# First tiles of a hash attention: full-height tables for the low parts, and another order of copies and loads

## Chip, core and metric

One NeuronCore of one Trainium2 chip runs the whole program. The metric is the device time of one execution in microseconds (us). Three executions of the kernel before took 699.73, 700.44 and 702.56 us; the median is 700.44 us.

## What is computed

Attention over 2 batches and 8 heads, 768 positions of 64 numbers each, where a query sees a key only if both fall into the same of 64 hash buckets; then two feed-forward blocks over the 1536 tokens. Cut to what matters here:

```
q_bits = (q @ proj > 0); k_bits = (k @ proj > 0)      # 6 bits
mask   = bucket(q_bits) == bucket(k_bits)
scores = where(mask, q @ k.T / 8, -1e9)
attn   = softmax(scores) ; x = attn @ v               # per head
x = (silu(x @ w_gate) * (x @ w_val)) @ w_out           # 512 -> 1536 -> 512
h = x @ w_in ; x = layernorm(h * softmax(h)) * g_ln @ w_out2
```

The feed-forward weights are 64-bit floats in memory and are turned to 32 bits by VectorE.

## The kernel before

**Numbers in two parts.** A float32 operand is kept as a rounded "high" part and a "low" rest, and products are summed from the parts. So each head's queries and keys, once transposed, stand in 128-row tiles: `kt` and `qa` hold high parts in rows 0 to 63 and low parts in rows 64 to 127. The score matmuls (`scores`, L515 to 528) read four other tiles: `ka` (the keys' high part twice), `qa`, `qb` (queries' high part, under it first the keys' high part and then the hash bits) and `kb` (the keys' low part, under it the hash bits).

**Pairs and slots.** Heads go in 8 pairs. A pair has 12 slots; slot i does one block of 128 queries against all 768 keys: `scores(i+1)`, `maxima(i)` and `biases(i)` on VectorE (DVE), `exps(i)` on ScalarE (ACT), the transposes of slot i-2 on TensorE (PE), their high and low parts on ACT and DVE (`highs`, `lows`), and the product with the values for slot i-5. `scores(i+1)` needs the PSUM buffer of `scores(i-1)`, so it starts after `exps(i-1)`. The order of all instructions is written by hand in the loop L797 to L847 and kept on each engine.

**Hashes of the first pair.** `first_hashes(j)` (L381 to 422) does one head at a time: 8 matmuls (L393) into two PSUM banks, four each, alternating between a table over all 128 rows (`hash_k`, `hash_q`) and one over the upper 64 rows only (`hash_first`, `hash_low`, rows `up`). Head 0 is done before the first score (in `start`), head 1 in slot 2, right behind the transposes of slot 0. DVE turns the sums into bits (L419, L403).

**Hashes of the other pairs.** `hashes(p, n)` (L467 to 494) does both heads of a pair in 6 matmuls (L483), three tables by two heads, all of 128 rows; the third table, `hash_low`, reads `qb`, in whose rows 0 to 63 lie the queries' high parts and in rows 64 to 127 the keys' high parts. They are put there by DMAs: `turn(p, j, g)` (L430 to 465) transposes a head's queries and keys in three groups, ACT copies them out, and for g = 1 four copies go out on SyncE's (SP's) DMA queue, `qb<-kt`, `ka<-kt` twice and `kb<-kt`, for g = 2 one more, `qb<-qa`. Each is 64 rows of 768 float32, 192 KB. For pair 1 these are the slots 3 to 6 of pair 0 (`beginning`), and its hashes are in slots 8 and 9. Slot 9's bits then go by four small DMAs (L494) into `qb` and `kb`; the first score of pair 1 is issued in slot 11.

**Loads and splits.** `load` (L232) brings a pair's queries, keys or values (384 KB each) on the same SP queue, into buffers of which there is one for each kind, so a load waits until GpSimd (POOL) has split the one before. In pair 0 the loads of pair 2's keys and queries, pair 1's values, pair 3's keys and queries stand in slots 2, 4, 6, 8, 10 (L770). POOL splits pair 1's keys and queries and pair 0's values by heads in 12 steps (`split_heads`, `opening`), of which one is taken in `start` and 2, 1, 2, 2, 2, 2 in slots 0 to 5 (L837).

**First weights.** `early` (L752) loads the first columns of `w_gate` and `w_val` (512 KB each) and converts them in 6 DVE steps each (L47 to L64). Its 14 steps are taken one before the loop (the first load, L789) and then one in each of the slots 3, 9 and 11 of every pair (L846) until they are done. The result is read when the attention has ended.

Of the kernel before, what the change touches and what calls it, by code (L numbers as in the profile page):

```python
# [9 lines left out]
F32 = mybir.dt.float32  # L10
# [57 lines left out]
def hash_attention_then_two_mlps(  # L68
# [116 lines left out]

    def window(w, g, rows=slice(0, P)):

        tile, start, _ = w
        return tile[rows, start - g * GR:start - g * GR + P]

# [17 lines left out]
    def hash_tables():  # L208
        start = hash_q[1]
        hash_fill(hash_q)  # L210
        nc.gpsimd.tensor_sub(pl, pj, hash_q[0][:, start:start + NB].bitcast(F32))
        hash_fill(hash_k, hash_first, hash_low)

    with at:
# [8 lines left out]

        hash_first = hash_weights(xs, "hash_first", 1, 3, (up, 0, 1, pl), tag="xf", bufs=3)
        one = sm.tile([P, 1], F32, tag="one", name="one", bufs=1)
# [155 lines left out]
        def first_hashes(j):  # L381
# [6 lines left out]
            for n in range(2):  # L388
                for m, (w, g, nm, rows) in enumerate((
                    (hash_k, 1, "kt", both), (hash_first, 1, "kt", up),  # L390
                    (hash_q, 0, "qa", both), (hash_low, 0, "qa", up),
                )):
                    nc.tensor.matmul(  # L393
                        t[n][:, :HALF], window(w, 2 * j + g, rows),
                        x[nm][rows, n * HALF:(n + 1) * HALF],
                        start=m == 0, stop=m == 3,
                    )
# [26 lines left out]
        def tiles_of_head():  # L424
# [3 lines left out]
            }  # L428

        def turn(p, j, g, bank=None):  # L430

# [21 lines left out]
            if g == 0:  # L453
                nc.scalar.mul(kt[:, 0:512], t, qscale)
            elif g == 1:
                nc.scalar.mul(kt[:, 512:S], t[:, 0:S - 512], qscale)
                nc.scalar.copy(qa[:, 0:1024 - S], t[:, S - 512:512])
                for dst, src in (
                    (qb[D:P], kt[0:D]), (ka[0:D], kt[0:D]), (ka[D:P], kt[0:D]),
                    (kb[0:D], kt[D:P]),  # L460
                ):
                    nc.sync.dma_start(dst.bitcast(F32), src.bitcast(F32))
            else:
                nc.scalar.copy(qa[:, 1024 - S:S], t)
                nc.sync.dma_start(qb[0:D].bitcast(F32), qa[0:D].bitcast(F32))

# [297 lines left out]
        def splitting(p, l):  # L764


            loads = {6: ((p + 3, "k"),), 9: ((p + 3, "q"),), 0: ((p + 1, "v"),)}
            at = {2: "k", 4: "k", 5: "q", 8: "q", 10: "v", 11: "v"}
            if p == 0:
                loads = {  # L770
                    2: ((p + 2, "k"),), 4: ((p + 2, "q"),), 6: ((p + 1, "v"),),
                    8: ((p + 3, "k"),), 10: ((p + 3, "q"),),
                }
                at = {6: "k", 7: "k", 8: "q", 9: "q", 10: "v", 11: "v"}
            for of in loads.get(l, ()):
                load(*of)
            nm = at.get(l)
            if nm:
                if nm not in splits:
                    splits[nm] = split(p + 1 if nm == "v" else p + 2, nm)  # L780
                    go(splits[nm])
                else:
                    go(splits.pop(nm))

        with tc.manual_schedule():
            for p, nm in ((1, "k"), (1, "q"), (0, "v")):
                load(p, nm)
            first_weights = early()
            go(first_weights)  # L789
            opening = (  # L790
# [6 lines left out]
            for i in range(NSLOT + 9):  # L797
# [38 lines left out]
                if i < 6:  # L836
                    for _ in range((2, 1, 2, 2, 2, 2)[i]):  # L837
                        go(opening)
# [4 lines left out]
                if part == 1:  # L843
                    go(done)
                    sums(h + 1)
                if l in (3, 9, 11):  # L846
                    go(first_weights)  # L847
# [397 lines left out]
```

## Time and profile before

| | us |
|---|---|
| median of three executions | 700.44 |
| the profiled execution | 700.14 |
| its span, first to last instruction | 698.30 |
| PE busy | 689.4 (99%) |
| DVE busy | 555.3 (80%) |
| ACT busy | 339.5 (49%) |
| POOL busy | 149.4 (21%) |

The rows that follow the change are of this one profiled execution. Times are from the start of the span. PE is matmuls, PEld the loading of their weights, SPq the DMA issues on SyncE's queue. "PEclk" is TensorE's granted clock as a share of 2.4 GHz. In a timeline row, the first number is the start, the second the time taken (of all the instructions merged into it, their count behind the x), and in brackets stands how long the engine sat idle before and what ended the wait. A matmul's given duration includes its way through the array; two that follow each other closely are better read by the distance of their starts.

### The profile page before, as it was taken

Reading aid. Unit: us, or ns where it says so; the run is one execution under the profiler, and the core shown is the slowest. Engines: PE = TensorE matmul, PEld = TensorE weight load, DVE = VectorE, ACT = ScalarE, POOL = GpSimd, SP = SyncE. Lnnn points to the kernel's source line nnn. Section 1 sums busy time; section 2 is a strip of 40 time slices with the busy share of each in tenths; the row PEclk is TensorE's granted clock in tenths of the full one; section 3 lists DMA queues with packets and bytes.
Section 4 is the critical chain, followed back from the end, with each engine's and each line's share of the span. In section 5 each row is a group of like instructions: output and inputs, shape, how many; then the busy total and the mean of one; then the engine's idle time right before and its main releaser. Section 6 shows DMA issues by size and latency. Waiting matters only on the chain.

```text
span 698.3 us, 10092 instructions
## 1 busy us (share of the span) xinstructions
PE 689.4 (99%) x3683; PEld 592.8 (85%) x3683; DVE 555.3 (80%) x979; ACT 339.5 (49%) x676; POOL 149.4 (21%) x156
## 2 busy tenths in 40 slices
PE   8899999999999999999999999999999999999998
PEld 5789999999999988888888888888888888888887
DVE  6779999999989998766786886977988976645552
ACT  6868989889898963433213122032123432222221
POOL 5626566555644260000000000000000000000000
PEclk9999999999999999999999999999999999999999
DMA  6745746446261403231313131131221000000001
GB/s 188 180 129 128 177 113 164 125 123 162 55 153 39 143 13 120 72 110 61 116 65 119 62 120 62 60 122 60 80 103 61 1 6 25 16 30 16 31 15 46
DMA packets 36177, 60.59 MB, mean 87 GB/s; under 512 B 4984, under 2 KB 26552, under 8 KB 35616
## 3 DMA queue, kind: packets, MB, share of 16 engines
q1 hardware_dynamic: 36128, 59.95, 29.7%
q8 instruction: 29, 0.48, 0.3%
q14 instruction: 20, 0.16, 0.1%
HBM read 36.71 MB, written 3.15 MB: 57 GB/s over the span
## 4 chain that ended last, share of the span: by engine, by line
PE 97%; ACT 2%; DMA 1%; issue 0%; DVE 0%; ACTq 0%
PE h L992 28%; PE s L524 10%; PE h L1104 10%; PE t L574 9%; PE y L1017 5%; PE y L1018 5%; PE y L1016 5%; PE av L609 5%; PE av L613 4%; PE o L1161 3%; PE o L1162 3%; PE o L1163 3%; PE pp L483 2%; PE t L1143 2%; PE pp L445 1%; DMA qb<-qa 1%
## 5 line engine op out<-in xcount | busy, mean ns | idle before, releaser
L992 PE MATMUL h<-xh,hi 128*128 128x512 f32 x288 | 112.2, 390 | 0.0
L992 PE MATMUL h<-xl,hi 128*128 128x512 f32 x288 | 112.2, 390 | 0.0
L992 PE MATMUL h<-xh,lo 128*128 128x512 f32 x288 | 111.3, 390 | 0.0
L587 DVE TENSOR_TENSOR el<-t,eh 128x384 fp32r<-128x384 f32 x192 | 97.9, 551 | 10.7 <-ACT eh L583 8.9
L559 ACT ACTIVATE e<-s,nm 128x768 f32<-128x768 f32 x96 | 97.9, 1020 | 4.4 <-PE s L524 2.2
L583 ACT CAST eh<-t 128x384 fp32r<-128x384 f32 x192 | 84.1, 495 | 25.3 <-PE t L574 23.9
L1130 POOL TENSOR_TENSOR w<-w,half 128x1 f32<-128x1 f32 x12 | 6.6, 550 | 416.2 <-DVE w L1129 322.0
L535 DVE TENSOR_REDUCE top<-s 128x1 f32<-128x768 f32 x96 | 90.7, 945 | 2.2 <-PE s L524 2.0
L574 PE MATMUL t<-idr,e 128*128 128x128 f32 x576 | 80.6, 275 | 0.0
L574 PEld LDWEIGHTS t<-idr,e 128*128 128x128 f32 x576 | 68.7, 141 | 8.7 <-DVE el L587 2.8
L609 PE MATMUL av<-eh,vs 128*128 128x384 f32 x186 | 64.6, 347 | 0.0
L992 PEld LDWEIGHTS h<-xh,hi 128*128 128x128 f32 x288 | 54.1, 188 | 11.2
L992 PEld LDWEIGHTS h<-xl,hi 128*128 128x128 f32 x288 | 54.1, 188 | 11.1
L992 PEld LDWEIGHTS h<-xh,lo 128*128 128x128 f32 x288 | 54.0, 188 | 11.1
L1002 ACT CAST ah<-sg 128x512 fp32r<-128x512 f32 x36 | 22.4, 622 | 74.6 <-DVE sg L1000 74.6
L524 PE MATMUL s<-ka,qa 128*128 128x384 f32 x192 | 55.4, 370 | 1.1 <-ACT e L559 1.1
L1017 PE MATMUL y<-al,hi 128*128 128x512 f32 x144 | 56.1, 390 | 0.0
L1018 PE MATMUL y<-ah,lo 128*128 128x512 f32 x144 | 56.1, 390 | 0.0
L1016 PE MATMUL y<-ah,hi 128*128 128x512 f32 x144 | 56.1, 390 | 0.0
L1000 DVE TENSOR_TENSOR sg<-h,sg 128x512 f32<-128x512 f32 x36 | 24.8, 690 | 37.0 <-PE h L992 22.0
L613 PE MATMUL av<-el,vs 128*64 128x384 f32 x155 | 52.8, 340 | 0.0
L963 ACT CAST hi<-wf 128x1024 fp32r<-128x1024 f32 x17 | 17.8, 1050 | 69.8 <-DVE wf L64 69.8
(212 smaller groups left out, 1427.9 us busy)
## 6 DMA issues: line engine op xcount, KB each, us to landing
raw<-in_moe_w_out_dram SPq DMA_DIRECT2D x10, 1024.0 KB
raw<-in_moe_w_gate_dram SPq DMA_DIRECT2D x12, 512.0 KB
raw<-in_moe_w_val_dram SPq DMA_DIRECT2D x12, 512.0 KB
ka<-kt SPq DMA_DIRECT2D x30, 192.0 KB
raw<-in_moe_w_in_dram SPq DMA_DIRECT2D x4, 1024.0 KB
v<-in_v_dram SPq DMA_DIRECT2D x8, 384.0 KB
kb<-kt SPq DMA_DIRECT2D x15, 192.0 KB
qb<-qa SPq DMA_DIRECT2D x15, 192.0 KB
```

Source lines behind the costliest of these rows:

```text
L524: nc.tensor.matmul(s[:, n, :HALF], a[:, rows], m[:, n * HALF:(n + 1) * HALF], start=first, stop=not first,)
L535: nc.vector.tensor_reduce(top[:, 1:2], s_of[i][:, :, :HALF], AX.XY, ALU.max, negate=True)
L559: nc.scalar.activation(e, s_of.pop(i)[:, :, :HALF], AF.Exp, bias=nm[:, 1:2], scale=nm[:, 0:1], accum_out=total_of[p, n][:, j, c:c + 1],)
L574: nc.tensor.transpose(t[:, m, :], e_of[i][:, g, m * P:(m + 1) * P], idf)
L583: nc.scalar.copy(half_tile(eh_of, i, g), t_of[i, g])
L587: last_of[i] = nc.vector.tensor_sub(half_tile(el_of, i, g), t_of.pop((i, g)), half_tile(eh_of, i, g).bitcast(F32),)
L609: nc.tensor.matmul(av, vj[:, c], eh_of[h][:, c, :], start=c == 0, stop=c == C - 1)
L613: nc.tensor.matmul(*low, start=False, stop=False)
L992: nc.tensor.matmul(ps[n], a[:, n, kk, :], x[:, kk, blk * BLK:(blk + 1) * BLK], start=kk == 0 and a is hi and x is xh, stop=kk == KD - 1 an ...
L1016: nc.tensor.matmul(p, hi[:, cols], ah, start=f == t * FT, stop=False)
L1017: nc.tensor.matmul(p, hi[:, cols], al, start=False, stop=False)
L1018: nc.tensor.matmul(p, lo[:, cols], ah, start=False, stop=f == (t + 1) * FT - 1)
```

## The change

The tables of the low parts for the first pair become two tiles of 128 rows, `hash_first["k"]` and `hash_first["q"]`, zero in rows 64 to 127, and all 8 matmuls of `first_hashes` read 128 rows. Of pair 1's copies, the three that `turn` issues for `ka` and `kb` of each head are kept in a list and issued behind the last `qb<-qa` of the pair. The loads in pair 0 move to slots 1, 4, 7, 9, 11. The splits' steps are taken 2, 1, 3, 2, 2, 1. The first load of `early` is not issued before the loop, and its steps are taken in slots 3, 9, 11 of pair 2 and later.

```diff
-    def window(w, g, rows=slice(0, P)):
+    def window(w, g):
         tile, start, _ = w
-        return tile[rows, start - g * GR:start - g * GR + P]
+        return tile[:, start - g * GR:start - g * GR + P]
...
-        hash_fill(hash_k, hash_first, hash_low)
+        hash_fill(hash_k, hash_first["k"], hash_first["q"], hash_low)
...
-        hash_first = hash_weights(xs, "hash_first", 1, 3, (up, 0, 1, pl), tag="xf", bufs=3)
+        hash_first = {
+            nm: hash_weights(xs, f"hash_first_{nm}", n, n + 2, (up, 0, n, pl), tag="xf", bufs=3)
+            for n, nm in enumerate("qk")
+        }
...
-                for m, (w, g, nm, rows) in enumerate((
-                    (hash_k, 1, "kt", both), (hash_first, 1, "kt", up),
-                    (hash_q, 0, "qa", both), (hash_low, 0, "qa", up),
+                for m, (w, g, nm) in enumerate((
+                    (hash_k, 1, "kt"), (hash_first["k"], 1, "kt"),
+                    (hash_q, 0, "qa"), (hash_first["q"], 0, "qa"),
                 )):
                     nc.tensor.matmul(
-                        t[n][:, :HALF], window(w, 2 * j + g, rows),
-                        x[nm][rows, n * HALF:(n + 1) * HALF],
+                        t[n][:, :HALF], window(w, 2 * j + g),
+                        x[nm][:, n * HALF:(n + 1) * HALF],
...
+        held = []
...
-                for dst, src in (
-                    (qb[D:P], kt[0:D]), (ka[0:D], kt[0:D]), (ka[D:P], kt[0:D]),
-                    (kb[0:D], kt[D:P]),
-                ):
-                    nc.sync.dma_start(dst.bitcast(F32), src.bitcast(F32))
+                move(qb[D:P], kt[0:D])
+                keys = [(ka[0:D], kt[0:D]), (ka[D:P], kt[0:D]), (kb[0:D], kt[D:P])]
+                if p == 1:
+                    held.extend(keys)
+                else:
+                    for dst, src in keys:
+                        move(dst, src)
             else:
                 nc.scalar.copy(qa[:, 1024 - S:S], t)
-                nc.sync.dma_start(qb[0:D].bitcast(F32), qa[0:D].bitcast(F32))
+                move(qb[0:D], qa[0:D])
+                if p == 1 and j == 1:
+                    for dst, src in held:
+                        move(dst, src)
...
                 loads = {
-                    2: ((p + 2, "k"),), 4: ((p + 2, "q"),), 6: ((p + 1, "v"),),
-                    8: ((p + 3, "k"),), 10: ((p + 3, "q"),),
+                    1: ((p + 2, "k"),), 4: ((p + 2, "q"),), 7: ((p + 1, "v"),),
+                    9: ((p + 3, "k"),), 11: ((p + 3, "q"),),
                 }
...
             first_weights = early()
-            go(first_weights)
...
-                    for _ in range((2, 1, 2, 2, 2, 2)[i]):
+                    for _ in range((2, 1, 3, 2, 2, 1)[i]):
                         go(opening)
...
-                if l in (3, 9, 11):
+                if p > 1 and l in (3, 9, 11):
                     go(first_weights)
```

## Rows read from the trace of the kernel before

**Rows 1.** The page, part 1: busy time, share of the span, instructions.

```profile
PE 689.4 (99%) x3683; PEld 592.8 (85%) x3683; DVE 555.3 (80%) x979; ACT 339.5 (49%) x676; POOL 149.4 (21%) x156
```

**Rows 2.** What PE waited for over the span: total us, times, longest.

```profile
PE pp L483 <- DMA qb<-qa: 3.2, 1, 3.2
```

**Rows 3.** Timeline of PE: pair 1's hashes and the scores behind them.

```profile
32.49 0.34 PE L483 MATMUL pp<-kt,hash_k 128*128 128x384 f32 x1
36.05 0.41 PE L483 MATMUL pp<-qb,hash_low 128*128 128x384 f32 x1 [3.23 <-DMA qb<-qa]
...
41.00 0.51 PE L524 MATMUL s<-ka,qa 128*128 128x384 f32 x2
...
46.15 0.51 PE L524 MATMUL s<-kb,qb 76*128 76x384 f32 x2
```

**Rows 4.** PE by stretches: us, PE busy (count), PEclk, DMA share, GB/s.

```profile
37.00:38.00 1.00, 1.00 (x5) 0.50 0.28 92
```

**Rows 5.** Timeline of PE: pair 2's hashes, the same instructions as rows 3.

```profile
62.70 0.33 PE L483 MATMUL pp<-kt,hash_k 128*128 128x384 f32 x1
62.87 0.33 PE L483 MATMUL pp<-qb,hash_low 128*128 128x384 f32 x1
...
66.14 0.51 PE L524 MATMUL s<-ka,qa 128*128 128x384 f32 x2
```

**Rows 6.** Stretch: PE, PEld, DVE, ACT, POOL busy; PEclk, DMA share, GB/s.

```profile
25.00:30.00 5.00, 4.87 (x34) 4.64 (x35) 4.10 (x8) 4.99 (x14) 3.26 (x4) 1.00 0.99 245
```

**Rows 7.** Timeline of PE: head 0's hashes, k transposes, first score.

```profile
6.17 0.41 PE L393 MATMUL pp<-kt,hash_k 128*128 128x384 f32 x1 [0.23 <-ACT kt L346]
6.51 0.43 PE L393 MATMUL pp<-kt,hash_first 64*128 64x384 f32 x1
...
9.10 0.88 PE L333 MATMUL t<-idr,first_ks 128*128 128x128 f32 x6
...
10.54 0.84 PE L524 MATMUL s<-kb,qb 76*128 76x384 f32 x2
```

**Rows 8.** Timeline of DVE: first load's wait, bits, first maximum, head 1's bits.

```profile
3.17 0.36 DVE L304 CAST first_ks<-first_k 128x384 fp32r<-128x384 f32 x1 [0.67 <-DMA first_k<-in_k_dram]
...
7.72 0.67 DVE L419 TENSOR_SCALAR kb<-pp,over,weigh 12x384 fp32r<-12x384 f32 x1 [0.40 <-PE pp L393]
...
9.21 0.67 DVE L419 TENSOR_SCALAR kb<-av,over,weigh 12x384 fp32r<-12x384 f32 x1 [0.26 <-PE av L393]
11.42 0.96 DVE L535 TENSOR_REDUCE top<-s 128x1 f32<-128x768 f32 x1 [1.54 <-PE s L524]
...
18.27 0.69 DVE L403 TENSOR_SCALAR bits<-av,over,weigh 64x384 fp32r<-64x384 f32 x1 [0.23 <-PE av L393]
```

**Rows 9.** Timeline of ACT: behind head 1's hashes, and pair 1's last copy.

```profile
19.49 0.86 ACT L583 CAST eh<-t 128x384 fp32r<-128x384 f32 x2 [1.86 <-PE t L574]
...
21.24 1.04 ACT L559 ACTIVATE e<-s,nm 128x768 f32<-128x768 f32 x1
...
27.91 0.68 ACT L464 CAST qa<-pp 128x512 fp32r<-128x512 f32 x1
```

**Rows 10.** DMA issues on SP's queue: start, time to issue.

```profile
14.55 0.46 SPq L286 DMA_DIRECT2D qb<-qa  x1
...
29.79 0.97 SPq L465 DMA_DIRECT2D qb<-qa  x1
...
42.74 0.77 SPq L286 DMA_DIRECT2D kb<-bits  x1
```

**Rows 11.** DMA share and GB/s of one stretch (PEclk first).

```profile
16.50:17.00 0.50, 1.00 0.10 25
```

**Rows 12.** The same queue: first bits copy of pairs 4, 5 and 6.

```profile
127.10 0.79 SPq L286 DMA_DIRECT2D qb<-bits  x1
...
157.00 0.79 SPq L286 DMA_DIRECT2D qb<-bits  x1
...
186.63 0.80 SPq L286 DMA_DIRECT2D qb<-bits  x1
```

## The prediction, made blind

> **What bounds the kernel now.** I read the busy times first: PE works 99% of the span [rows 1], so the time can only fall where PE waits, or where it is busy with less than it could do. What it waited for shows one long wait: the third table's matmul of pair 1's hashes, for the copy `qb<-qa` [rows 2]. The timeline there shows it: five matmuls follow at about 0.175 us, the fifth at 32.49, the sixth at 36.05 instead of 32.66 [rows 3], 3.4 us late. Behind the wait PE's clock is granted at half, 1.2 instead of 2.4 GHz [rows 4]. From the sixth matmul to the first score behind the second group takes 4.95 us (36.05 to 41.00) [rows 3]; the same instructions in the next pair, at full clock, take 3.27 us (62.87 to 66.14) [rows 5]. So the wait costs 3.4 us and 1.7 us more.
>
> Before the wait, in slots 3 to 8, ACT is the bound: 4.99 us of 5 busy, the DMA engines at 99% and 245 GB/s [rows 6]. Before that, PE is busy with little: the 8 matmuls of `first_hashes` start 0.34 to 0.38 us apart (6.17, 6.51, to 9.10 for the next work) [rows 7], those of `hashes`, as wide, 0.17 us [rows 5]. What differs is that each second one of the first uses 64 rows. Behind 41 us PE is without gaps, and what arrives there earlier arrives earlier at the end.
>
> **The change part by part.** The sum is made against the profiled execution, 700.14 us (span 698.30, 1.84 around it); the median of the three runs is 0.30 above it.
>
> *Tables of 128 rows, head 0.* Eight matmuls take 2.93 us (6.17 to 9.10) [rows 7]; at 0.175 us [rows 5] they take 1.4, so PE is 1.5 us ahead. DVE can't follow all the way: of its waits for these sums, 0.40 and 0.26 us fall away [rows 8], so its bits are done at 9.22 instead of 9.88. Score 0's second half needs the last of them; it starts at 9.3 instead of 10.54 [rows 7]. The maximum started 0.88 us behind that (11.42) [rows 8], with PE at half speed: the two matmuls there take 0.84 us, later ones 0.51 [rows 7, 3]. At half speed again the maximum comes at 10.2, 1.2 us earlier; at full speed at 9.8, 1.6 earlier. The slow end is the row itself; I take 1.3, between 1.0 and 1.6.
>
> *The same tables, head 1.* Again 1.5 us less on PE. Behind them ACT had idled 1.86 us for the transposes [rows 9], so it starts 1.5 earlier. But DVE's second set of bits waited only 0.23 us for PE [rows 8], so it comes only that much earlier, at 18.04 to 18.73, and pair 1's first transposes, which go into the same bank, wait for it: 18.8 us, then 0.4 for them and 0.8 for ACT's last two copies ahead of its exponential, which starts at about 20.1 instead of 21.24 [rows 9]. Taken: 1.2, between 0.9 and 1.5. All of this is in the old time scale; the 1.3 of head 0 comes on top. From here to 33 us ACT has no gap to lose it in [rows 6], so slots 3 to 8 move up by 2.5 us.
>
> The price of the tables is a DVE memset like the three beside it, in DVE's 0.67 us of waiting for the first load [rows 8], and one more small POOL block ahead of `hash_low`, which the first pair no longer reads. POOL's low part of head 0's successor slips by the length of one such block, and has its reader, the transposes, at 7.6 instead of 9.10 [rows 7]; it is ready by then. Without this cover it would be some 0.2 us. The two tiles take two of the three `xf` buffers until slot 2, the first `xf` is written in slot 8: nothing.
>
> *The copies and loads.* The last `qb<-qa` was issued at 29.79 [rows 10], 1.2 us behind the end of ACT's copy at 28.59 [rows 9], since SP was still issuing key copies; and it landed 6.3 us later, since everything in front of it had to go first. From the load in slot 2 on, these were 2 loads of 384 KB, 6 key copies and, with itself, 4 `qb` copies of 192 KB: 2688 KB. The change leaves 1152 KB of them: the 4 `qb` copies and one load. The missing 1536 KB take 6.4 us at 245 GB/s [rows 6]. By the queue alone the copy lands at 29.6 in the old scale; by its issue, at 28.59 and with the 2.1 us that a lone copy took (issued at 14.55, the engines idle from 16.6 on) [rows 10, 11], at 30.7. Its reader is due at 32.66. Both scales move up by 2.5 us alike, so a margin of 2 us stays, and the 3.4 us go altogether; with them the 1.7 us of half clock. Bounds: 0 to 5.1; I take all, because the margin is as large as a lone copy's whole time.
>
> *What is late next.* The 6 held copies are issued behind it, some 0.7 us each, from 26.7 to 31 in new time, and behind them on SP wait pair 1's values and `low<-xf`, neither read for several slots. 1152 KB and the load take 6.4 us, and are through at about 34.6. Pair 1's first score reads `kb` at 46.15 [rows 3], in new time 38.5. Ahead of it lie only slot 9's bits: `kb<-bits` was issued at 42.74 [rows 10], 3.4 us before its reader, and keeps this distance. So 3 us of room, and nothing charged; if it is gone, PE stands at that score.
>
> *Moved steps.* The key load of slot 1 is issued when POOL has split the keys before, and SP's next issue, head 1's bits, waits longer. A POOL step moves from slot 5 up to slot 2, where POOL waits for the next bias anyway. The conversions leave pairs 0 and 1 and come into pairs 5 and 6: a pair with three of them took 29.90 us, the next, without, 29.63 [rows 12]. As many leave as come; 0, between -0.5 and +0.5. The second of the weights' loads now has only slots 9 to 11 of pair 4 to land in, near 5 us against 2.1 and its transfer; if that is too little, DVE stands for up to 1 us.
>
> Sum: 1.3 + 1.2 + 3.4 + 1.7 = 7.6, so 692.5 beside the profiled run, and with 0.3 for the median 692.8.
>
> **The rivals.** *Height does not matter.* The eight matmuls stay 0.37 us apart, because the cause is something else, the two banks for one, and the 2.5 us don't come. For it: no row shows the first pair's hashes at 128 rows. Against it: tables, columns and types are those of rows 5, and the 64-row form is the one difference I see. The wait and its clock still go: 5.1 us, 695.3. The Trainium skill speaks for this rival: "TensorE: Matmul & The Clock Gate", in its section "Why this matters for your kernels", says that a matmul over 32 rows takes the time of one over 128, and that the gain of few rows lies in running several at once. By that rule the sum would be 5.1; the rows' 0.37 against 0.17 us speak against it.
>
> *The wait moves.* The held copies or the bits behind them land late, and PE stands at pair 1's first score. For it: six copies in one burst, at full DMA load. Against it: the 3 us of room. It would take 1 to 3 us back: 694 to 696.
>
> *The copy is still late.* The order in the queue is not what makes it late, and the change does not do what it is for; only the tables count: 700.4 - 2.5 = 697.9. Against it: the DMA engines were at 99% while it waited [rows 6], with just what the change takes out from in front of it.
>
> *Slower: half clock in slots 3 to 8.* With the hashes done in half the time PE waits for DVE and ACT from 17 us on, and its clock may be granted at half there, as it was behind the wait in rows 4. A slot's work then takes PE 3.6 us, as 36.05 to 39.65 did (the end is where the second group of hashes starts, 1.35 us ahead of 41.00 at the measured pace) [rows 3], where ACT needs 2.25, six slots from its 19.49 [rows 9] to about 33: 1.35 us a slot, and once PE is the bound again, behind slot 8, the full difference of a stretch such as rows 3 and 5 show, 1.7. Eight slots of it cost 6 times 1.35 and 2 times 1.7, 11.5 us, so 704; it decides from about five slots on, where the 7.6 us are eaten up. Against it: in 25 to 30 us PE waits as much already and the clock is full [rows 6].
>
> **How the numbers follow.** The forecast with all four terms has 0.78; height 0.06; the moved wait 0.07; the copy still late 0.05; slower 0.04. Its own bounds are 1.0 + 0.9 + 5.1 - 0.5 = 6.5 to 1.6 + 1.5 + 5.1 + 0.5 = 8.7 us, so 691.7 to 693.9; with the spread of runs 691.2 to 694.2. To hold the first two rivals the range goes up to 696.0, and it goes down to 690.8 for a clock that is full from the start. A change of less than 0.5%, 3.5 us, can't well be told from none here. The first three cases are faster by more than that, the fourth is not, and some of the forecast's mass may go with unseen mishaps: faster 0.88, no change 0.08, slower 0.04.
>
> **What would show it.** Right: starts 0.17 to 0.2 us apart in both `first_hashes`; DVE's maximum of slot 0 at 9.8 to 10.2; no wait of PE for `qb<-qa`, and full clock from 30 to 40 us; the first bits copy of pair 1 at 34 to 35 instead of 41.90; the same distance from there to the end. Wrong: starts still 0.37 apart (height), a wait of PE for `ka`, `kb` or bits at the first score of pair 1, a wait in pair 1's hashes, half clock from 17 us on, or pairs 5 and 6 longer than 29.9 us.

## The result, and the profile after

The changed kernel's median is 693.52 us (693.10 to 694.72, five executions) beside 701.30 us (699.73 to 704.53) for the kernel before on the same chip, a ratio of 0.9888 [0.9858, 0.9918]. The forecast was 692.8, range 690.8 to 696.0, faster with 0.88. The profiled execution took 693.10 us with a span of 691.2, 7.1 less than the 698.30 of before.

Lines of code in the profiles of the changed kernel stand 3 to 10 further down than in those of before (L393 is now L396, L483 is L493, L524 is L534, L286 is L289); in the experiments they lie between.

The busy times, answering to [rows 1]:

```profile
PE 684.1 (99%) x3683; PEld 589.4 (85%) x3683; DVE 554.8 (80%) x980; ACT 340.4 (49%) x676; POOL 150.3 (22%) x157
```

PE still works 99% of the span. It has 5.3 us less of busy time for the same 3683 matmuls, so most of the gain is matmuls that take less time, and not idle time alone. What PE still waits for, longest first (total, times, longest), answering to [rows 2]:

```profile
PE s L534 <- ACT e L569: 1.5, 2, 1.3
PE t L380 <- DVE signs L175: 1.2, 1, 1.2
PE pp L396 <- POOL hash_low L197: 0.4, 1, 0.4
```

The wait for `qb<-qa` is gone from the list, and no copy has taken its place.

**Head 0.** PE's timeline of `first_hashes`, and what follows it, against [rows 7]:

```profile
6.01 0.42 PE L396 MATMUL pp<-kt,hash_k 128*128 128x384 f32 x1 [0.42 <-POOL hash_low L197]
6.27 0.33 PE L396 MATMUL pp<-kt,hash_first_k 128*128 128x384 f32 x1
6.44 0.39 PE L396 MATMUL pp<-qa,hash_q 128*128 128x384 f32 x1
...
7.55 0.62 PE L336 MATMUL t<-idr,first_ks 128*128 128x128 f32 x6
```

The eight now take 1.54 us (6.01 to 7.55) where they took 2.93. DVE's timeline, against [rows 8]:

```profile
9.62 0.96 DVE L545 TENSOR_REDUCE top<-s 128x1 f32<-128x768 f32 x1 [0.53 <-PE s L534]
```

ACT's timeline, against [rows 9]:

```profile
16.15 0.86 ACT L593 CAST eh<-t 128x384 fp32r<-128x384 f32 x2 [0.32 <-PE t L584]
...
18.11 0.99 ACT L569 ACTIVATE e<-s,nm 128x768 f32<-128x768 f32 x1
```

The first maximum starts at 9.62 instead of 11.42, 1.80 us earlier. The exponential behind head 1's hashes starts at 18.11 instead of 21.24, 3.13 us earlier, so head 1 adds 1.33. ACT's idle time for the transposes fell from 1.86 to 0.32.

**Pair 1.** Its hashes on PE, answering to [rows 3]:

```profile
29.46 0.35 PE L493 MATMUL pp<-kt,hash_k 128*128 128x384 f32 x1
29.65 0.34 PE L493 MATMUL pp<-qb,hash_low 128*128 128x384 f32 x1
...
32.94 0.52 PE L534 MATMUL s<-ka,qa 128*128 128x384 f32 x2
...
38.11 0.52 PE L534 MATMUL s<-kb,qb 76*128 76x384 f32 x2
```

The fifth matmul comes 3.03 us earlier than before, the sixth 0.19 us behind it instead of 3.56, and the score behind the second group at 32.94 instead of 41.00: 8.06 us. The first score of pair 1 (38.11) waits for nothing. By stretches (PE, PEld, DVE, ACT and POOL busy with counts; PEclk, DMA share, GB/s), against [rows 4, 6]:

```profile
25.00:26.00 1.00, 1.00 (x7) 0.89 (x6) 1.00 (x3) 1.00 (x3) 1.00 (x1) 1.00 0.09 28
...
27.00:28.00 1.00, 1.00 (x8) 0.92 (x7) 0.96 (x3) 1.00 (x3) 1.00 (x1) 1.00 0.93 203
...
26.00:37.00 11.00, 11.00 (x76) 10.54 (x75) 9.94 (x21) 8.51 (x20) 6.80 (x5) 1.00 0.75 179
```

The clock is granted in full through the stretch in which it was at half. At 25 us the DMA engines are almost idle (0.09), where they had been at 99%: the last `qb<-qa` meets empty queues. The held copies fill them from 27 us on. SP's issues, answering to [rows 10, 12]; the last line is the first fetch of the feed-forward weights:

```profile
25.58 0.46 SPq L289 DMA_DIRECT2D qb<-qa  x1
26.09 1.23 SPq L289 DMA_DIRECT2D ka<-kt  x2
...
33.90 0.79 SPq L289 DMA_DIRECT2D qb<-bits  x1
...
178.63 0.81 SPq L289 DMA_DIRECT2D qb<-bits  x1
...
208.53 0.79 SPq L289 DMA_DIRECT2D qb<-bits  x1
...
218.74 0.37 SPq L926 DMA_DIRECT2D raw<-in_moe_w_gate_dram  x1
```

The lead over the kernel before is 8.00 us at the first bits copy of pair 1 (41.90 to 33.90), again 8.00 at that of pair 6 (186.63 to 178.63), 7.74 at that of pair 7 (216.27 to 208.53) and 7.15 at the fetch (225.89 to 218.74). It stays so to the end. So 0.85 us are given back late in the attention, 0.26 in one pair and 0.59 in the 10 us behind it. There the last conversion of the first weights stands on DVE:

```profile
212.99 0.68 DVE L64 CUSTOM_DVE_ANT_0 w1f<-raw,w1f 128x1024 uint16<-128x1024 uint16 x1
213.59 0.95 DVE L545 TENSOR_REDUCE top<-s 128x1 f32<-128x768 f32 x1
```

DVE is without gaps there, and the scores around it start at 211.43, 213.50 and 216.02: a slot of 2.07 us, and with the conversion in it one of 2.52. That is 0.45 of the 0.59 us.

### The profile page after: what moved, and what is told of

Read it like the earlier page. It is cut to its first block, busy times and chain, and to the rows that moved or that the text cites. A ratio compares the mean times of both kernels' runs of the same rounds, so it can differ in the third digit from the quotient of the medians.

```text
span 691.2 us, 10096 instructions
## 1 busy us (share of the span) xinstructions
PE 684.1 (99%) x3683; PEld 589.4 (85%) x3683; DVE 554.8 (80%) x980; ACT 340.4 (49%) x676; POOL 150.3 (22%) x157
## 4 chain that ended last, share of the span: by engine, by line
PE 96%; DVE 2%; ACT 1%; issue 0%; ACTq 0%; DVEq 0%
PE h L1001 28%; PE h L1113 10%; PE s L534 10%; PE t L584 9%; PE y L1025 5%; PE y L1026 5%; PE y L1027 5%; PE av L619 5%; PE av L623 4%; PE o L1170 3%; PE o L1171 3%; PE o L1172 3%; PE pp L493 2%; PE pp L450 2%; PE t L1152 2%; PE pp L652 1%
## 5 line engine op out<-in xcount | busy, mean ns | idle before, releaser
L534 PE MATMUL s<-ka,qa 128*128 128x384 f32 x192 | 54.6, 365 | 1.7 <-ACT e L569 1.5
```

The costliest lines, as they stand in the source:

```text
L534: nc.tensor.matmul(s[:, n, :HALF], a[:, rows], m[:, n * HALF:(n + 1) * HALF], start=first, stop=not first,)
```

## The experiments

The theory has three parts: the tables give 2.5 to 3 us because alternating heights cost PE time; the held copies alone take away the wait and its half clock; the other loads, splits and weights give nothing. The rivals are that height does not matter, that the moved loads and not the order of the copies empty the queue, and that the lead is lost by something other than the conversions. Each kernel is named by what it does; times are medians in us, ratios to the kernel before beside it on the same chip.

| kernel | median (lowest to highest), executions | ratio |
|---|---|---|
| tables_alone | 698.26 (696.54 to 700.71), 9 | 0.9955 [0.9939, 0.9972] |
| order_alone | 696.39 (694.14 to 702.06), 10 | 0.9938 [0.9907, 0.9968] |
| loads_alone | 702.98 (697.46 to 704.50), 10 | 1.0008 [0.9976, 1.0039] |
| rows_grouped | 699.93, 1 | |
| all_but_tables | 700.36 (694.88 to 703.51), 10 | 0.9963 [0.9931, 0.9994] |
| all_but_order | 697.79 (695.96 to 699.10), 10 | 0.9936 [0.9916, 0.9955] |
| all_but_loads | 693.90 (693.26 to 694.82), 4 | 0.9891 [0.9861, 0.9922] |
| weights_from_pair1 | 695.15 (694.22 to 696.16), 6 | 0.9909 [0.9884, 0.9935] |
| changed_again | 694.42 (693.00 to 694.58), 5 | 0.9905 [0.9889, 0.9921] |
| weights_joined | 693.08 (692.47 to 694.43), 6 | 0.9896 [0.9879, 0.9912] |
| all_but_weights | 692.40 (692.38 to 693.60), 4 | 0.9888 [0.9872, 0.9905] |
| load_first_steps_pair1 | 692.22 (692.13 to 693.49), 6 | 0.9861 [0.9835, 0.9887] |

### One part alone

**tables_alone**, the kernel before with the tables of 128 rows:

```diff
-                    (hash_k, 1, "kt", both), (hash_first, 1, "kt", up),
-                    (hash_q, 0, "qa", both), (hash_low, 0, "qa", up),
+                    (hash_k, 1, "kt"), (hash_first["k"], 1, "kt"),
+                    (hash_q, 0, "qa"), (hash_first["q"], 0, "qa"),
```

> The kernel before with the 128-row tables alone. If the height is what spaces the matmuls, their starts are 0.17 to 0.2 us apart, slots 3 to 8 move up by 3.0 us (1.8 from head 0, 1.2 from head 1, as the trace of the changed kernel has it), and the wait for the last qb copy stays about as long, since its queue moves up with the slots: 3.0 us faster. Rival: the copy's queue does not move up, because its first entry, the key load of slot 2, is held by something else; then the wait eats the gain and less than 1 us is left.

Measured: the eight matmuls of head 0 start from 6.30 to 7.71, the next work at 7.89, so 1.59 us. PE's timeline at pair 1's hashes:

```profile
29.89 0.33 PE L486 MATMUL pp<-kt,hash_k 128*128 128x384 f32 x1
33.82 0.66 PE L486 MATMUL pp<-qb,hash_low 128*128 128x384 f32 x1 [3.60 <-DMA qb<-qa]
...
40.04 0.61 PE L527 MATMUL s<-ka,qa 128*128 128x384 f32 x2
```

And the stretch behind it (columns as above):

```profile
35.00:38.00 3.00, 3.00 (x14) 2.71 (x12) 1.32 (x3) 0.28 (x1) 0.90 (x1) 0.50 0.06 18
```

The fifth matmul comes 2.60 us earlier than before (32.49 to 29.89) and the sixth 2.23 (36.05 to 33.82); the wait has grown a little. Then half clock lasts longer: from the sixth to the score it takes 6.22 us where it took 4.95, and of the lead 0.96 us are left at the score (41.00 to 40.04) and 0.9 in the span (698.3 to 697.4). By the medians the gain is 3.4 us (701.62 to 698.26). The 3 us ahead of the wait are shown; what is left of them at the end hangs on how long the clock stays at half, and that differs between executions.

**order_alone**, the kernel before with the held copies:

```diff
+                move(qb[D:P], kt[0:D])
+                keys = [(ka[0:D], kt[0:D]), (ka[D:P], kt[0:D]), (kb[0:D], kt[D:P])]
+                if p == 1:
+                    held.extend(keys)
...
+                if p == 1 and j == 1:
+                    for dst, src in held:
+                        move(dst, src)
```

> The kernel before with the six key copies of pair 1 held back, nothing else. If the bytes in front of the last qb copy make it late, 1536 of 2688 KB are left in front of and in it, at 215 GB/s (2688 KB from 23.2 to 36.05 us) 7.3 us, so it lands at about 30.5, before its reader at 32.66: no wait, no half clock, 5.1 us faster. Rival: the loads' move is what frees the queue and the order is of little use; then a wait of 1 us or more stays here and the gain is under 3 us.

Measured: six of ten executions took 694.14 to 697.25, the other four 700.21 to 702.06. The profiled one is of the second kind (700.46). PE's timeline of it, at head 1's hashes and at pair 1's:

```profile
16.97 0.67 PE L393 MATMUL pp<-kt,hash_k 128*128 128x384 f32 x1
17.57 0.69 PE L393 MATMUL pp<-kt,hash_first 64*128 64x384 f32 x1
...
37.61 0.35 PE L490 MATMUL pp<-kt,hash_k 128*128 128x384 f32 x1
37.80 0.34 PE L490 MATMUL pp<-qb,hash_low 128*128 128x384 f32 x1
```

And a stretch ahead of the second pair of lines:

```profile
24.00:25.00 1.00, 1.00 (x8) 1.00 (x6) 0.96 (x3) 0.63 (x2) 0.20 (x1) 0.50 0.22 37
```

The wait is gone (0.19 us between the fifth and the sixth), as expected. But PE ran at half clock from between 8 and 9 us to between 25 and 26, and its 64-row hashes start 0.60 us apart instead of 0.37. So the fifth matmul comes 5.1 us later than before (37.61 to 32.49), as much as the wait and its half clock gave back. By the medians the gain is 5.2 us (701.62 to 696.39), as expected. The six short executions lie around 695.0, which is the 700.14 of before less 5.1; none of them was profiled. In the profiled one the copy's reader comes 5.1 us late itself, so the clean test of the order is all_but_loads, further down.

**loads_alone**, the kernel before with the loads' slots, the splits' steps and the weights' steps:

```diff
-                    2: ((p + 2, "k"),), 4: ((p + 2, "q"),), 6: ((p + 1, "v"),),
+                    1: ((p + 2, "k"),), 4: ((p + 2, "q"),), 7: ((p + 1, "v"),),
...
-                if l in (3, 9, 11):
+                if p > 1 and l in (3, 9, 11):
```

> The kernel before with the loads' slots, the splits' steps and the first weights moved, the copies and tables as they were. By bytes: 2304 KB stay in front, 11 us from 23.2, so the copy lands at about 34.2 and 1.5 of the 3.4 us of wait go; half clock stays or is shorter; the conversions in pairs 6 and 7 take 0.85 us back: 0.5 to 2.5 us faster. Rival (the loads free the queue): no wait, 4 us faster or more.

Measured: nothing that can be told from none, where 0.5 to 2.5 us were expected. PE's timeline:

```profile
6.20 0.66 PE L393 MATMUL pp<-kt,hash_k 128*128 128x384 f32 x1 [0.23 <-ACT kt L346]
6.79 0.69 PE L393 MATMUL pp<-kt,hash_first 64*128 64x384 f32 x1
```

Again the hashes are 0.61 us apart, and PE is at half speed until about 27 us, so everything ahead of the wait is later, and only 0.73 us of the wait are left. This run therefore does not tell what the loads do to the queue; all_but_loads does.

**rows_grouped**, the kernel before with the 128-row matmuls of each bank ahead of its 64-row ones:

```diff
-                    (hash_k, 1, "kt", both), (hash_first, 1, "kt", up),
-                    (hash_q, 0, "qa", both), (hash_low, 0, "qa", up),
+                    (hash_k, 1, "kt", both), (hash_q, 0, "qa", both),
+                    (hash_first, 1, "kt", up), (hash_low, 0, "qa", up),
```

> The kernel before with the four matmuls of a sum reordered: the two of 128 rows first, then the two of 64 rows; tables and data as they were. If each change between heights costs about 0.2 us, 4 of the 8 distances of starts fall from 0.37 to about 0.17 us, and the eight take 2.2 us instead of 2.93. Rival: a matmul of 64 rows costs it by itself, whatever stands before it; then the sum of the eight does not change, or those behind 64 rows stay at 0.37. The time is 0 to 1.5 us shorter.

Measured, PE's timeline:

```profile
7.35 0.34 PE L393 MATMUL pp<-qa,hash_low 64*128 64x384 f32 x1
7.62 0.44 PE L393 MATMUL av<-kt,hash_k 128*128 128x384 f32 x1
7.90 0.34 PE L393 MATMUL av<-qa,hash_q 128*128 128x384 f32 x1
8.16 0.43 PE L393 MATMUL av<-kt,hash_first 64*128 64x384 f32 x1
```

The eight take 2.42 us (6.29 to the next work at 8.71), between the 2.93 of [rows 7] and 1.54. Head 1's eight take 2.16 (14.02 to 16.18), where they took 2.94 in the kernel before (15.21 to 18.15). With half as many changes of height, the mean distance of head 1's starts falls from 0.37 to 0.27 us, half of the way to 0.175. That fits a price of 0.19 us for each change of height, and none for the height itself. Against this reading seems to stand that the distances are all alike, 0.26 to 0.28, and not long at the changes alone. The loading of the weights (PEld) shows where the changes are:

```profile
15.63 0.18 PEld L393 LDWEIGHTS av<-kt,hash_first 64*128 64x128 f32 x1 [0.25 <-issue]
15.74 0.19 PEld L393 LDWEIGHTS av<-qa,hash_low 64*128 64x128 f32 x1
```

The matmuls of these two start at 15.64 and 15.92. The second has the height of the one before it, and its weights are loaded 0.18 us ahead of it. The first comes behind a matmul of 128 rows: PEld sits idle for 0.25 us, and loading and matmul start together. It is the same at all four changes of head 1 here, and at all eight in the kernel before (15.56 to 18.15).

Not every change of height has this price. The score matmuls of 76 rows follow those of 128, here in the changed kernel, two and two as in rows_grouped:

```profile
14.91 0.52 PE L534 MATMUL s<-ka,qa 128*128 128x384 f32 x2
15.27 0.52 PE L534 MATMUL s<-kb,qb 76*128 76x384 f32 x2
```

The next work starts at 15.62: four matmuls in 0.71 us, 0.18 each. So what is shown is a price of going between 64 and 128 rows. The Trainium skill, "TensorEngine Tiling (Array Packing)", section "Key Properties", says that changing the tiling mode drains TensorE; that agrees in kind, and it gives no time. The rows bound the rule on a second side: the products with 64 columns (128*64) that stand between those of 128 start 0.17 us apart, so a change of columns showed no price here.

The time of this one execution, 699.93, lies within the spread of the kernel before. The wait for `qb<-qa` is 4.4 us in it, so what the hashes gained was lost there.

### The change without one part

**all_but_tables**, the changed kernel with the 64-row tables of before:

```diff
-                    (hash_k, 1, "kt"), (hash_first["k"], 1, "kt"),
-                    (hash_q, 0, "qa"), (hash_first["q"], 0, "qa"),
+                    (hash_k, 1, "kt", both), (hash_first, 1, "kt", up),
+                    (hash_q, 0, "qa", both), (hash_low, 0, "qa", up),
```

> The changed kernel with the first pair's hashes as they were, half of them over 64 rows. If these rows set the clock at the start, as in the profiles of the two kernels with 64 rows whose matmuls ran at half speed up to 24 and 27 us, then here too some executions have long stretches at half speed and others not: 3 us slower than the changed kernel where the stretch is short (the 3.0 us that slots 3 to 8 moved up), 7 to 10 where it is long, and no wait for the last qb copy. Rival: the first weights' load, which is gone from the start, or the loads' order brings the half speed; then the next kernels, which share these moves, show it too although their rows are 128.

Measured: 700.36 by the median, with executions from 694.88 to 703.51; the profiled one (703.51) has no wait for `qb<-qa` and hashes 0.61 us apart from 6.21 on, at half speed until about 27 us. Its shortest execution is 1.8 us above the shortest of the changed kernel, its longest 8.8 above the longest. Six of the ten took 699.38 or more. So the tables' worth is not their 3 us alone: without them the profiled execution runs its first 27 us at half speed, and the other long ones, not profiled, probably do too.

**all_but_order**, the changed kernel without holding the copies:

```diff
-                if p == 1:
-                    held.extend(keys)
-                else:
-                    for dst, src in keys:
-                        move(dst, src)
+                for dst, src in keys:
+                    move(dst, src)
```

> The changed kernel without the holding back of the key copies. By bytes: 2304 KB in and in front of the last qb copy, from about 20.4 us at 215 to 245 GB/s, so it lands at 30.0 to 31.4 with its reader due at 29.65: a wait of 0.4 to 1.7 us and perhaps no half clock; 0.4 to 2 us slower than the changed kernel (693.5). Rival: the order is what counts and not the loads; then the wait is 3 us or more, with half clock behind it, 4 to 5 us slower.

Measured: 4.3 us more than the changed kernel by the medians (3.9 more than all_but_loads, which ran on the same chip), 4.8 by the spans (696.0 to 691.2). PE's timeline:

```profile
29.49 0.33 PE L486 MATMUL pp<-kt,hash_k 128*128 128x384 f32 x1
...
32.57 0.66 PE L486 MATMUL pp<-qb,hash_low 128*128 128x384 f32 x1 [2.75 <-DMA qb<-qa]
```

The stretches:

```profile
25.00:26.00 1.00, 1.00 (x7) 0.92 (x7) 1.00 (x3) 1.00 (x3) 1.00 (x1) 1.00 0.89 290
26.00:27.00 1.00, 1.00 (x10) 0.96 (x9) 0.81 (x2) 1.00 (x4) 0.25 (x2) 1.00 1.18 250
...
31.00:32.00 1.00, 0.00 (x0) 0.00 (x0) 0.00 (x0) 0.00 (x0) 0.00 (x0) 1.00 0.98 203
```

More than the theory gave. The sixth matmul comes 2.92 us later than in the changed kernel (32.57 to 29.65), and half clock behind it costs 1.60 more (4.89 us to the score at 37.46, where it is 3.29). The last `qb<-qa` is issued only 0.8 us later (26.37 to 25.58), but into queues that are full until 32 us, where the changed kernel's row for 25 to 26 us showed 0.09. Against tables_alone, from which it differs by the loads, the splits and the weights alone, the sixth matmul is late by 2.90 us instead of 3.75. That is 0.85 us for the load that no longer lies in front of the copy, but it is not clear of chance: three profiles with the old order and the old loads have 3.39 (the kernel before), 3.75 (tables_alone) and 4.53 (rows_grouped). What the moved load is worth is therefore not shown; what the six held copies are worth is, by the next kernel.

**all_but_loads**, the changed kernel with the loads in their old slots:

```diff
-                    1: ((p + 2, "k"),), 4: ((p + 2, "q"),), 7: ((p + 1, "v"),),
-                    9: ((p + 3, "k"),), 11: ((p + 3, "q"),),
+                    2: ((p + 2, "k"),), 4: ((p + 2, "q"),), 6: ((p + 1, "v"),),
+                    8: ((p + 3, "k"),), 10: ((p + 3, "q"),),
```

> The changed kernel with the loads of pair 0 in their old slots. 1536 KB in and in front of the last qb copy need 6.4 to 7.3 us from about 20.4 us, so it lands by 27.7, before 29.65: no wait, the changed kernel's time within 0.3 us. Rival: the loads' move is needed as well; then a wait of up to 1.5 us.

Measured: 693.90 and a span of 691.2, the changed kernel's own; no wait came back. The moved loads give nothing that can be measured; the order of the copies alone takes the wait away, whole, with PE at full clock and its reader on time (the fifth matmul at 29.54, the sixth at 29.72).

### Where the 0.85 us went

**weights_from_pair1**, the changed kernel with the weights' steps a pair earlier:

```diff
-                if p > 1 and l in (3, 9, 11):
+                if p > 0 and l in (3, 9, 11):
```

> The changed kernel with the first weights' steps from pair 1 on instead of pair 2. The changed kernel loses 0.85 us of its lead between 42 and 226 us: 0.26 in the pair whose slots have the conversion's fourth and fifth steps of the second weights, 0.59 in slots of 2.06 us behind the last hashes, where DVE is the bound and the last step (0.68 us) falls. One pair earlier no step falls there: 0.5 to 0.85 us faster than the changed kernel. Rival: the loss sits elsewhere, or pair 1 takes as much; then no difference.

Measured: slower, 695.15, and a span of 694.3, 3.1 above the changed kernel's. SP's issues:

```profile
123.42 0.53 SPq L242 DMA_DIRECT2D q<-in_q_dram  x1
124.01 0.49 SPq L766 DMA_DIRECT2D raw<-in_moe_w_val_dram  x1
```

DVE's timeline:

```profile
131.38 0.43 DVE L47 TENSOR_SCALAR w1f<-raw 128x512 int32<-128x512 int32 x1 [2.42 <-DMA raw<-in_moe_w_val_dram]
```

The second weights' load, issued in slot 9, falls behind a load of queries, and its first conversion two slots later stands 2.42 us. PE waits for DVE 1.8 us behind it, and is then granted half clock from 134 to 137 us. From the first bits copy of the pair to that of the next it takes 33.26 us (119.50 to 152.76), where the changed kernel takes 29.89 (119.05 to 148.94). So much more is lost here than the 0.85 us that the earlier steps could give. The same load is in the changed kernel issued at 153.44 and read at 158.33, without a wait; the same conversion waited 0.6 us in loads_alone, 1.0 in all_but_tables, 0.3 in all_but_order.

**changed_again**, the changed kernel, beside the next:

> The changed kernel once more, beside the two that follow. Theory: its second load of the first weights is issued in slot 9 and read in slot 11, and just lands in time or up to 1 us late; so its times spread over some 1.5 us, 693 to 695, and where the profile shows a wait of DVE for this load, the time is at the upper end.

Measured: two levels, 693.00 and 693.01, then 694.42 to 694.58. The profiled execution is of the lower (693.00, span 690.9), without a wait for the weights' load. No profile of an upper one was had, so the load as their cause is not shown; load_first_steps_pair1 points to another.

**weights_joined**, steps from pair 1 on, the second load as the end of the first weights' last conversion:

```diff
-                yield
+                if n:
+                    yield
...
-                if p > 1 and l in (3, 9, 11):
+                if p > 0 and l in (3, 9, 11):
```

> The changed kernel with the first weights' steps from pair 1 on, and the second load issued in the same slot (3) as the first weights' last step, so six slots lie between this load and its first use and the last step falls in slot 3 of pair 5. No DVE wait for a load, no step behind the last hashes: the 0.85 us between 42 and 226 us stay, and the half clock of the run before does not come. 0.5 to 1.2 us faster than the changed kernel beside it. Rival: the loss of the run before came from the steps in pairs 1 to 3, not from the late load; then it is slower than the changed kernel again.

Measured: 693.08, which is 1.3 us under changed_again by the medians, but 0.5 above it by the spans (691.4 to 690.9), so that it is faster is not shown. The conversions don't wait for their loads any more. But the first load, 512 KB issued at 50.27 in slot 3 of pair 1, now lies in front of pair 2's key and query copies, and PE waits 0.8 us for `qb<-qa` there. A wait gone and another one come.

**all_but_weights**, the changed kernel with the first weights as in the kernel before (the first load ahead of the loop, steps from pair 0 on):

```diff
             first_weights = early()
+            go(first_weights)
...
-                if p > 1 and l in (3, 9, 11):
+                if l in (3, 9, 11):
```

> The changed kernel with the first weights as in the kernel before: first load ahead of the loop, steps from pair 0, last one in pair 4. No late load, no step in pairs 5 and 6, so the 0.85 us stay; against it one DVE step of 0.42 us in slot 3, where DVE is busy 4.87 of 5 us, and 512 KB more in the queue at the start. 0.3 to 0.9 us faster than the changed kernel. Rival: the load at the start delays head 1's copies or the step in slot 3 delays the hashes, and it is no faster or slower.

Measured: 692.40, with a span of 690.5, beside 694.42 and 690.9 for changed_again. SP's issues, the copy and the fetch between which the changed kernel lost 0.59 us:

```profile
208.45 0.79 SPq L289 DMA_DIRECT2D qb<-bits  x1
...
218.08 0.37 SPq L927 DMA_DIRECT2D raw<-in_moe_w_gate_dram  x1
```

The stretch takes 9.63 us, as it did before the change (9.62), and not 10.21. From the first bits copy (34.19) to the fetch the lead does not fall: 7.71 us there, 7.81 here. The other profiles agree: with the step in this stretch it takes 10.20 us (changed_again) and 10.21 (all_but_loads), without it 9.62 or 9.63 (weights_from_pair1, weights_joined, load_first_steps_pair1). So the 0.85 us are the conversions put off to pairs 5 and 6. Putting them back is not free: the first bits copy of pair 1 comes 0.29 us later than in the changed kernel (33.90 to 34.19), so 0.66 us are left at the fetch.

**load_first_steps_pair1**, the first load ahead of the loop, steps from pair 1 on:

```diff
             first_weights = early()
+            go(first_weights)
...
-                if p > 1 and l in (3, 9, 11):
+                if p > 0 and l in (3, 9, 11):
```

> The changed kernel with the first weights' first load ahead of the loop again, and its steps from pair 1 on. The second load then falls in slot 3 of pair 3, six slots ahead of its first use, the last step in slot 3 of pair 5; no step lies in pair 0, no load beside pair 2's copies in pair 1. No wait of DVE or PE for a load, none of the 0.85 us lost behind 42 us: 692 to 692.6, a span of about 690.2, as the kernel with the first weights of before (692.4, span 690.5) or 0.3 better. Rival: the steps in pairs 1 and 2 cost what those in pairs 5 and 6 did; then 693 or more.

Measured: the lowest time of all, 692.22, a ratio of 0.9861, though not apart from all_but_weights by their intervals. Five of its six executions took 692.13 to 692.31 (spans 690.3 to 690.5); the sixth, the profiled one, 693.49 (span 691.6). PE's timeline of that one, head 0's hashes and head 1's:

```profile
7.29 0.52 PE L396 MATMUL pp<-qa,hash_first_q 128*128 128x384 f32 x1
7.61 0.52 PE L396 MATMUL av<-kt,hash_k 128*128 128x384 f32 x1
...
15.08 0.34 PE L396 MATMUL pp<-qa,hash_q 128*128 128x384 f32 x1
15.25 0.34 PE L396 MATMUL pp<-qa,hash_first_q 128*128 128x384 f32 x1
```

Here, with 128 rows, head 0's hashes start 0.32 us apart and head 1's 0.17. The work behind head 0 starts at 8.88 instead of 7.55 in the changed kernel. These 1.3 us are the distance between this execution and the other five. all_but_loads and all_but_weights also have two levels, 1.2 us apart, and changed_again 1.4; that these are the same is likely and was not seen. The lead is not lost in the weights' steps here: from the first bits copy of the last pair to the fetch of the next weights it takes 9.62 us (209.58 to 219.20).

## Why the prediction was right, and where it was not

*The bound.* Right: what moved the end was the one wait of [rows 2], its half clock and the stretch ahead of it, and from 33 us to pair 6 the lead stays at 7.8 to 8.1 us.

*The tables.* Right in kind, 0.5 us too small. Starts of 0.17 to 0.18 us came as said. Head 0 gave 1.80 where 1.3 (1.0 to 1.6) was taken: the clock was full behind the hashes, so that the maximum came at 9.62, even a little before the 9.8 that the text gave for this, and the hashes began 0.16 us earlier than before. Head 1 gave 1.33 for 1.2. At pair 1's hashes it is 3.03 for 2.5. Whether POOL had its tables ready in time stays open: in this execution the profile names POOL as what released the first hash matmul [0.42 <-POOL hash_low], though no matmul of `first_hashes` reads `hash_low` any more, and in six others with these tables it names ACT's `kt`, with the start at 5.8 to 6.2 us.

*The rival that height does not matter* fell with tables_alone and with the rows: 0.175 us for 0.37. The rule that the prediction cited from the Trainium skill ("TensorE: Matmul & The Clock Gate", section "Why this matters for your kernels") concerns one matmul by itself. There the trace agrees: in rows_grouped a matmul of 64 rows behind another of 64 takes 0.34 us, as one of 128 behind 128 does. What has a price is the change between the two heights.

*The copy.* Right to 0.1 us: 3.37 us of the wait and 1.66 of the half clock (4.95 to 3.29 us from the sixth matmul to the score) for 3.4 and 1.7. The 99% that it gives for the DMA engines "while it waited" is the row of 25 to 30 us, ahead of the wait; in the wait itself, from 33 to 36 us, the share is 1.03 to 1.09, so the reading holds. But the argument that counted bytes at one rate, 245 GB/s, was wrong in what it made of the parts. Counted so, all_but_order should have waited 0.4 to 1.7 us; it was 2.9 us late. Counted so, the load that is taken out from in front of the copy is worth 1.6 us (384 KB); all_but_order has some 0.85 for it, not clear of chance, and all_but_loads shows that the copy is in time without that (which the count had said too). The rates say why in part. The held copies, alone in the queues from 27 to 28 us of the changed kernel, went at 203 GB/s at a share of 0.93; the first loads of the kernel before, from 9 to 10 us, at 395 GB/s at 1.06. By these rates, as an estimate, a copy of 192 KB takes 0.97 us, and a load of twice its bytes 1.0. The copies go from tile to tile and have 64 rows, the loads come from the inputs and have 128; no run here tells which of the two makes the copies slow.

*What is late next.* Right: the held copies were issued from 26.09 to 30.28, the first score of pair 1 came at 38.11 (38.5 was said) without a wait. The rivals that the wait moves there, and that the copy is still late, fell with the changed kernel's waits.

*Slower by half clock in slots 3 to 8* did not come: PEclk is 1.00 from 26 to 37 us, and in every microsecond from 17 to 26 as well. Half clock over these slots came instead in runs with 64-row hashes, where PE has hardly a gap (order_alone, 8 to 25 us: busy for 16.56 of 17 us); the prediction did not foresee it.

*The conversions.* This is the term that failed: "As many leave as come; 0, between -0.5 and +0.5". It was -0.85. In pairs 0 and 1 the conversions had cost little (0.29 us up to pair 1's bits in all_but_weights, the first load included), and in pairs 5 and 6 they cost 0.26 and 0.59. The prediction had the row for the first (29.90 us with three of them, 29.63 without [rows 12]) and let the pairs that they leave cancel it. The last slots of pair 6, where DVE is without gaps, it did not look at. The warning about the second load's two slots was right in kind: it just fits in the changed kernel, and costs up to 3.4 us in weights_from_pair1.

*The sum.* 3.03 + 3.37 + 1.66 - 0.85 = 7.2 us beside the 7.1 of the spans, where 7.6 was said: 0.5 too little for the tables, 0.85 too much for the conversions, so that two errors in part cancelled, by luck.

## What to carry to other kernels

Matmuls of 64 rows that alternate with those of 128 cost TensorE more than the rows they save; a zero-filled table of full height is cheaper, here by 1.4 us for eight matmuls. Matmuls of 76 rows showed no such price. When one transfer is late behind a full queue, put what is needed later behind it; counting bytes does not tell which of those in front counts, since the copies of 64 rows from tile to tile moved at about half the rate of the loads of 128. Work on a second engine that is "only moved" is free where that engine has room and has its full price where it has none, so look at the slots it comes into one by one.

## What was not expected of the hardware

Half clock over long stretches went with the 64-row hashes. In five profiles with them, PE was at half speed until 25 to 27 us in three (order_alone, loads_alone, all_but_tables), for some 3 us behind head 0's hashes in the kernel before, and not in rows_grouped; in nine with 128 rows only load_first_steps_pair1 shows any between the first hash and 25 us, up to about 10. The spread of the times goes the same way: the changed kernel lies between 693.0 and 694.7 in all its executions, the kernel before between 697.1 and 705.1. Not all of that spread is the start: tables_alone, with 128 rows and the wait still there, lies between 696.5 and 700.7. Part of the gain by the medians is probably that the long executions are gone. That the clock follows the height of the tables rests on these profiles and on all_but_tables, which differs from the changed kernel by the tables alone; why it does is open.

The granted clock of the first microseconds is no witness: in loads_alone PEclk reads 1.00 from 6 to 11 us while the matmuls start 0.61 us apart, and in load_first_steps_pair1 it reads 1.00 at 0.32. Starts of 128-row matmuls 0.32 us apart for 384 columns are half speed (tables_alone has them from 38.44 to 40.04, where PEclk reads 0.50), 0.175 full; alternating heights give 0.61 and 0.37. There the distance of the starts has to be read in place of the clock's row.
